# Attention with always-kept keys, then an FFN, on one core: one product per pair of heads for the kept keys

## The chip, the cores and the metric

One core of a Trainium2 chip. The metric is device time in microseconds (us) of one execution of the whole program. Before the change the median of 3 runs is 654.59 us (654.31 to 654.69).

## What is computed

Attention over 4 batches, 8 heads, 768 positions, head size 64, in fp32, where a query sees the keys of a window of 128 positions back from itself and, always, the first `n_sink` = 4 keys of the sequence (the kept keys). Then an FFN over the 3072 tokens:

```python
keep = is_sink | in_window
a = softmax(where(keep, scale * q @ k.T, -1e9))
x = (a @ v) laid out as [B * S, H * D]       # 3072 x 512
h = x @ w_in                                  # 512 -> 2048
g = h * clip(h + 3, 0, 6) / 6
out = g @ w_out                               # 2048 -> 512
```

## The kernel before

**Tiling.** The work is cut into 12 units of 256 positions (4 batches, 3 units each) and 4 pairs of heads, so 48 slots, each a pair of heads in a unit. The first 16 slots are the first units of the four batches. They have no earlier keys and so no separate kept keys, and run by an order written out by hand (`FIRST`, L734) together with loading the FFN's weights. The other 32 slots, called pairs below, run by the list `ORDER` (L858), one round of it per slot; stages of up to three slots are in work at once, as in a software pipeline. The letter f in `ORDER` takes the next step of the FFN for two units that are already done.

```python
ORDER = "f s f c00 c01 k c10 f e0 q c11 f e1 f l v d0 f f d1 f"
```

TensorE gets its instructions in this order. In this part the builder orders VectorE and ScalarE by what is ready, earlier steps first.

**Precision.** Products that need full fp32 precision are made from fp32r parts: a value is split into a high part and the rest (`split_parts`, L27, one copy and one subtraction), and the products of the parts are added up in PSUM.

**A pair's steps.** c (L385) makes four score products sp (head 0 or 1, two tiles of 128 queries each); for each VectorE's custom reduction (L382) reads sp out of PSUM, adds the mask and takes the smallest. ScalarE makes the exponentials with their sums (L419), VectorE the reciprocals (L444, L445), POOL joins two blocks (L461), ScalarE normalizes (L407). For the second head VectorE also copies the probabilities of the kept keys of both heads, high and low parts, into `ssc` (L470). d (`D_pt`, L484) transposes a head's probabilities on TensorE into pt, splits them into ph (copy on ScalarE, subtraction on VectorE, L35 and L30), and POOL masks the parts (L507, L509).

s (`D_snk`, L512) transposes `ssc` into PSUM (spt), from where ScalarE copies two blocks of 64 rows x 128 columns into `pz` (L521). The rest of `pz` is zero and stays so: POOL cleared it once (L224, in `later_constants`). Rows 0 to 63 of `pz` go with the first 128 queries, rows 64 to 127 with the second; in either half the rows hold high and low parts for both heads.

e (`E_av`, L533) multiplies one head's ph by the value parts. The 128 stationary columns `vsl` are that head's value parts, high in columns 0 to 63 and low in 64 to 127, so the result av[:, 0] has the high values' share on rows 0 to 63 and the low values' share on rows 64 to 127; av[:, 1] holds what the low probabilities add. Four matmuls (256 columns each) do that, and a fifth adds the kept keys: `sinks(p)[:, vsl]` by `pz` (L557). Then ScalarE copies rows 64 to 127 into the result x (L561) and VectorE adds the other two parts, 64 rows each (L562, L563).

`sinks(p)` (L234) holds the kept keys' values for a pair of heads, 4 x 64 columns: high and low parts of both heads, split from `raw_s` (`sink_loads`, L239; 16 times, once per batch and pair of heads). Its 128 rows are 8 groups of 16 kept keys, where a group has the values of one head and zeros for the other.

**The FFN between.** A step f is half a first product hps (six matmuls of 512 columns, L688, in `two_product`; the second half is followed by the activation on ScalarE and VectorE, L620 to L634), or a second product (`two_second`, L691; six matmuls, L698) into the sums o of a unit. With 8 f per slot, 8 slots take the 64 steps of two units.

**PSUM.** All PSUM tiles of the stretch come from one pool `ps` of eight banks (L58), under one tag, "bank". A tile has its bank from its first matmul until its last reader is done. The four sums o (two units, two tiles of 128 rows) are held from their first second product to the output, nearly all of eight slots. All others (sp, pt, spt, av, hps) take turns in the banks that are left.

After the last pair the FFN of the last two units runs alone. At the end a branch, not taken with these inputs, covers other window sizes.

Of the kernel before, what the change touches and what calls it, by code (L numbers as in the profile page):

```python
# [9 lines left out]
F32 = mybir.dt.float32  # L10
F32R = mybir.dt.float32r
# [3 lines left out]
ALU = mybir.AluOpType  # L15
# [3 lines left out]
P = 128  # L19
SK = 16  # L20
# [6 lines left out]
def split_parts(nc, hi, lo, src, hi_engine, lo_engine):  # L27

    copy_r(nc, hi_engine, hi, src)
    lo_engine.tensor_tensor(out=lo, in0=src, in1=hi.bitcast(F32), op=ALU.subtract)  # L30


def copy_r(nc, eng, out, src, scale=1.0):
    if eng is nc.scalar:
        nc.scalar.mul(out=out, in_=src, mul=scale)  # L35
    elif eng is nc.gpsimd:
        nc.gpsimd.tensor_scalar(out=out, in0=src, scalar1=scale, scalar2=1.0, op0=ALU.mult, op1=ALU.mult)
    elif scale != 1.0:
        nc.vector.tensor_scalar(out=out, in0=src, scalar1=scale, scalar2=None, op0=ALU.mult)
    else:  # L40
        nc.vector.tensor_copy(out=out, in_=src)  # L41
# [3 lines left out]
def attn_ffn_kernel(ctx: ExitStack, tc: tile.TileContext, qx, kx, vx, px, vsx, limits, w_in, w_out, out):  # L45
    nc = tc.nc
    B, NU, NP = qx.shape[0:3]
    NT, DM = out.shape
    NFP = w_in.shape[0]
    H, D, UT = 2 * NP, 64, 256  # L50
# [6 lines left out]
    work = fast.enter_context(tc.tile_pool(name="work", bufs=2))  # L57
    ps = fast.enter_context(tc.tile_pool(name="ps", bufs=8, space=PSUM))  # L58
# [53 lines left out]
    def outside(dst, src, limit):  # L112
        nc.vector.tensor_scalar(out=dst, in0=src, scalar1=limit, scalar2=-BIG, op0=ALU.is_ge, op1=ALU.mult)
# [101 lines left out]
    pz = work.tile([P, UT], F32R, name="pz", bufs=1)  # L215

    def later_constants():

        nc.gpsimd.tensor_copy(out=m_t0[:, P:2 * P], in_=ownb)
        outside(m_t0[:, 2 * P:W2], colf[:, 0:SK], ns_f)  # L220
        nc.gpsimd.tensor_copy(out=m_t1[:, 0:P], in_=m_t0[:, 0:P])
        nc.gpsimd.tensor_copy(out=m_t1[:, P:P + SK], in_=m_t0[:, 2 * P:W2])
        nc.gpsimd.tensor_copy(out=m_t1[:, P + SK:W2], in_=m_t0[:, P:2 * P])
        nc.gpsimd.memset(pz.bitcast(F32), 0.0)  # L224

    kept = {}

# [5 lines left out]

    def sinks(p):  # L234
        if "vs" not in kept:
            kept["vs"] = work.tile([P, NP, 4 * D], F32R, tag="w0", name="vs", bufs=1)
        return kept["vs"][:, p]

    def sink_loads(s):  # L239
        b, u, p = pus[s]  # L240
        if p == 0:
            kept["raw_s"] = work.tile([P, NP, 2, D], F32, name="raw_s", bufs=1)
            nc.sync.dma_start(out=kept["raw_s"], in_=vsx[b])
        v4 = sinks(p).rearrange("p (h d) -> p h d", h=4)
        split_parts(nc, v4[:, 0::2, :], v4[:, 1::2, :], kept["raw_s"][:, p], nc.scalar, nc.vector)

    SSE = "DD"
    START = 9
# [22 lines left out]
    def plain(s):  # L271
        return s < NF32 and pus[s][1] == 0
# [83 lines left out]
    def by_tile(x):  # L356

        return x.rearrange("p (a s t) -> p a t s", s=2, t=P // 2)
# [63 lines left out]
    def R_plain(s):  # L422
        d = st_[s]
        nc.vector.tensor_scalar(out=d["sm"], in0=d["av"][:, :, D], scalar1=1e-9, scalar2=None, op0=ALU.add)
        nc.vector.reciprocal(out=d["rc"], in_=d["sm"])

    def U_plain(s):
        d = st_[s]
        d["rows"] = work.tile([P, 2, 2, D], F32, tag="tmp", name="rows", bufs=1)
        nc.vector.tensor_tensor(out=d["rows"].rearrange("p t h d -> p h t d"),  # L430
                                in0=d["av"][:, :, 0:D].rearrange("p (h t) d -> p h t d", h=2),
                                in1=d["rc"].rearrange("p (h t) -> p h t", h=2).unsqueeze(3).to_broadcast([P, 2, 2, D]),
                                op=ALU.mult)

    def V_plain(s):
        d = st_[s]
        d["xp"] = ps.tile([P, UT], F32, tag="bank", name="xp")
        for t in range(2):
            nc.tensor.transpose(out=d["xp"][:, t * P:(t + 1) * P],
                                in_=d["rows"][:, t].rearrange("p h d -> p (h d)"), identity=ident)  # L440
# [71 lines left out]
    def D_snk(s):  # L512
        b, u, p = pus[s]
        if not u:
            return
        d = st_[s]
        sp = ps.tile([P, 512], F32, tag="bank", name="spt")
        nc.tensor.matmul(out=sp[:, 0:P], lhsT=ssc, rhs=ident_r, start=True, stop=True)
        for t in range(2):
            rows = slice(4 * SK * t, 4 * SK * (t + 1))  # L520
            nc.scalar.copy(out=pz[rows, t * P:(t + 1) * P], in_=sp[rows, 0:P])  # L521

    def E_plain(s, h):
        d = st_[s]
        if h == 0:
            d["av"] = ps.tile([P, 4, D1], F32, tag="bank", name="av")
        for t in range(2):
            for slot in range(t + 1):
                c = (t + slot) * P
                nc.tensor.matmul(out=d["av"][:, 2 * h + t, :], lhsT=d["pf"][:, h, c:c + P], rhs=d["VS"][:, slot, h, :],  # L530
                                 start=(slot == 0), stop=(slot == t))

    def E_av(s, h):  # L533
        b, u, p = pus[s]
        d = st_[s]
        VS = d["VS"]
        ops = [(1, P, 0, UT), (0, 0, 0, P), (2, 3 * P, P, UT)] if u else [(0, 0, 0, UT), (1, 2 * P, P, UT)]
        if plain(s):
            E_plain(s, h)
            if h == 1:  # L540
                R_plain(s)
                U_plain(s)
                V_plain(s)
                x_high(s, d["xp"])
            return

        av = ps.tile([P, 2, UT], F32, tag="bank", name="av")
        vsl = slice(2 * D * h, 2 * D * (h + 1))
        seq = []
        for slot, c, o0, o1 in ops:  # L550
            if o1 - o0 == P:
                r = d[f"pt{h}"][:, :, c:c + P].rearrange("p r (s t) -> p r t s", s=2)
                seq.append((VS[:, slot, vsl], r, av[:, :, o0:o1]))
            else:
                seq += [(VS[:, slot, vsl], by_tile(d[f"pt{h}"][:, r, c:c + UT]), av[:, r, :]) for r in range(2)]
        if u:
            seq.append((sinks(p)[:, vsl], by_tile(pz), av[:, 0, :]))  # L557
        for j, (l, r, o) in enumerate(seq):
            nc.tensor.matmul(out=o, lhsT=l, rhs=r, start=(j == 0), stop=(j == len(seq) - 1))  # L559
        rows = x_whole(s)[D * h:D * (h + 1)]  # L560
        nc.scalar.copy(out=rows, in_=av[D:P, 0, :])  # L561
        nc.vector.tensor_tensor(out=rows, in0=av[0:D, 1, :], in1=rows, op=ALU.add)  # L562
        nc.vector.tensor_tensor(out=rows, in0=av[0:D, 0, :], in1=rows, op=ALU.add)  # L563

    def in_rows(x):

        return x.rearrange("p (a t s) -> p a t s", s=2, t=P // 2)

    def x_whole(s):
        if "xf" not in kept:  # L570
            kept["xf"] = work.tile([P, 2 * NP, UT], F32, tag="sb0", name="xf", bufs=1)
        return kept["xf"][:, s % (2 * NP)]
# [15 lines left out]
    def x_high(s, src):  # L588
        if s < 2 * NP:
            copy_r(nc, weng(XHF, s), in_rows(x_two(s)[:, 0, s // NP % 2]), by_tile(src))  # L590
        else:
            copy_r(nc, weng(XHF, s), in_rows(x_whole(s)), by_tile(src))
# [217 lines left out]
    def first_step(step):  # L810
        kind, *n = step.split(".")
        n = [int(x) for x in n]
        if kind == "i":
            keep_busy(n[0], ident)
        elif kind == "m":
            later_constants()
        elif kind == "M":
            S_least(*n, st_[n[0]]["sp", n[1], n[2]])
        elif kind == "x":
            x_high(n[0], st_[n[0]]["xp"])  # L820
        elif kind == "y":
            x_low(n[0], st_[n[0]]["xp"])
        elif kind == "b":
            x_split(*n)
        elif kind in pair:
            pair[kind](*n)
        else:
            unit_step(kind, *n)
# [32 lines left out]
    def order(s):  # L861
# [3 lines left out]
        return steps  # L865

    STEPS = {"l": A_kq, "v": A_v, "k": B_k, "q": B_q, "d": D_pt, "s": D_snk, "e": slot_E}

    queues.append(two_steps(1))
# [32 lines left out]
    with tc.If(flag == 1):  # L902
        with ExitStack() as gen:
# [76 lines left out]
            with tc.For_i(0, B, 1) as bi:  # L980
                for u in range(NU):
                    xn = gp.tile([P, NP, UT], F32, name="xn")
                    for c in range(NP):
                        nc.sync.dma_start(out=xn[:, c, :],
                                          in_=xv[ds(bi, 1), :, c, u * UT:(u + 1) * UT].rearrange("o p s -> (o p) s"))
# [73 lines left out]
```

## Time and profile before

| | |
|---|---|
| median of 3 runs | 654.59 us (654.31 to 654.69) |
| the profiled execution | 655.52 us |
| its span, first to last instruction | 653.8 us |
| TensorE busy (matmul) | 642.1 us, 98% |
| VectorE busy | 506.8 us, 78% |
| ScalarE busy | 399.6 us, 61% |
| POOL busy | 180.0 us, 28% |

PE is TensorE's matmul row, PEld its weight loads (each matmul has one), DVE is VectorE, ACT ScalarE, SP the queue that issues the transfers. L12 is line 12 of the kernel. In a timeline a row is a run of like instructions: start, duration, engine, line, operation, out<-in, shapes, count, and in brackets the idle time of the engine ahead of it with what ended that. Matmuls overlap: the duration of one is longer than the time until the next starts. The share of a whole span hides that stages differ; the stage in which the changed code runs is what counts.

### The profile page before, as it was taken

What the parts mean: (1) busy time and instruction counts of PE and PEld (TensorE: products, weight loads), DVE (VectorE), ACT (ScalarE), POOL (GpSimd) and SP (SyncE); (2) the same over time, 40 slices, a digit from 0 to 9 for tenths busy, and PEclk for the clock granted to TensorE, in tenths of its full rate; (3) what the DMA queues carried; (4) which work ended last, traced back from release to release, by engine and by line L of the source; (5) the groups of instructions that cost most, each with busy time, mean ns of one, the idle gap of its engine ahead of it and who ended that gap; (6) DMA issues with size and microseconds to landing.
All of it is one profiled execution on the core that took longest, in us unless ns stands there. A gap on an engine that the chain in (4) does not pass through costs nothing.

```text
span 653.8 us, 11574 instructions
## 1 busy us (share of the span) xinstructions
PE 642.1 (98%) x3556; PEld 574.6 (88%) x3556; DVE 506.8 (78%) x1353; ACT 399.6 (61%) x982; POOL 180.0 (28%) x336
## 2 busy tenths in 40 slices
PE   8999999999999999999999999999999999999996
PEld 7898988888888888899998999999899999888885
DVE  5999999957887888887889888879897887533331
ACT  4977778645776778766667766667866665311111
POOL 1000000002454354354444444544454344000000
PEclk9999999999999999999999999999999999999999
DMA  8455930017664656544454645444744440100001
GB/s 323 190 183 208 388 149 1 2 53 211 170 175 123 170 138 197 146 122 120 116 144 120 188 127 144 118 121 122 205 116 120 109 116 2 65 1 1 0 1 69
DMA packets 45749, 82.93 MB, mean 127 GB/s; under 512 B 7024, under 2 KB 30832, under 8 KB 43632
## 3 DMA queue, kind: packets, MB, share of 16 engines
q1 hardware_dynamic: 45680, 82.11, 43.1%
q8 instruction: 31, 0.51, 0.3%
q14 instruction: 38, 0.31, 0.1%
HBM read 41.19 MB, written 6.29 MB: 73 GB/s over the span
## 4 chain that ended last, share of the span: by engine, by line
PE 86%; ACT 4%; DVE 3%; DMA 2%; SPq 1%; issue 1%; POOL 1%; ACTq 0%; DVEq 0%; POOLq 0%
PE o L698 34%; PE hps L688 33%; PE av L559 5%; PE sp L400 4%; PE av L530 2%; PE pt L494 2%; PE sp L369 2%; PE o L643 2%; PE pt L476 1%; DMA vr<-in_vx_dram 1%; DMA qr<-in_qx_dram 1%; ACT Pt L407 1%; ACT Ph L417 1%; SPq L335 1%; PE idle L86 1%
## 5 line engine op out<-in xcount | busy, mean ns | idle before, releaser
L688 PE MATMUL hps<-x,w 128*128 128x512 f32 x1104 | 263.8, 383 | 0.0
L698 PE MATMUL o<-w,gh 128*128 128x512 f32 x736 | 223.9, 384 | 0.0
L688 PEld LDWEIGHTS hps<-x,w 128*128 128x128 f32 x1104 | 200.9, 189 | 25.2 <-ACT xf L35 0.3
L698 PEld LDWEIGHTS o<-w,gh 128*128 128x128 f32 x736 | 137.4, 197 | 11.2 <-issue 0.3
L698 PE MATMUL o<-w,g 128*128 128x512 f32 x368 | 139.7, 380 | 0.0
L461 POOL TENSOR_TENSOR Pt<-Pt 128x256 f32<-128x256 f32 x64 | 53.7, 839 | 276.3 <-ACT Pt L419 276.2
L620 ACT ACTIVATE ost<-hps,three 128x512 f32<-128x512 f32 x80 | 54.8, 685 | 83.4 <-PE hps L688 82.8
L625 DVE SCALAR_TENSOR_TENSOR ost<-ost,hps 128x512 f32<-128x512 f32 x80 | 54.5, 682 | 54.7 <-ACT ost L620 54.4
L507 POOL TENSOR_SCALAR_AFFINE_SELECT ph<-ph 128x256 fp32r<-128x256 f32 x128 | 66.6, 521 | 55.3 <-ACT ph L35 55.2
L698 PEld LDWEIGHTS o<-w,g 128*128 128x128 f32 x368 | 72.4, 197 | 7.0
L419 ACT ACTIVATE Pt<-Pt,nb 128x272 f32<-128x272 f32 x128 | 65.8, 515 | 19.7 <-DVE nb L382 16.7
L382 DVE CUSTOM_DVE_ANT_0 Pt<-sp,m_t 128x272 f32<-128x272 f32 x128 | 53.1, 431 | 25.8 <-PE sp L400 22.9
L509 POOL TENSOR_SCALAR_AFFINE_SELECT ph<-ph 128x256 fp32r<-128x256 f32 x128 | 61.0, 477 | 37.2 <-DVE ph L30 29.3
L407 ACT ACTIVATE Pt<-Pt,rc 128x144 f32<-128x144 f32 x128 | 46.2, 407 | 30.4 <-DVE rc L445 20.1
L634 DVE TENSOR_TENSOR g<-ost,gh 128x512 fp32r<-128x512 f32 x80 | 57.6, 720 | 2.6
L400 PE MATMUL sp<-K 128*128 128x272 f32 x256 | 41.8, 281 | 1.3 <-DVE ph L30 0.6
L400 PEld LDWEIGHTS sp<-K 128*128 128x128 f32 x256 | 37.6, 190 | 4.2 <-DVE ph L30 1.5
L559 PEld LDWEIGHTS av<-ph,VS 128*128 128x128 f32 x256 | 38.0, 190 | 3.6 <-issue 0.7
L559 PE MATMUL av<-ph,VS 128*128 128x256 f32 x256 | 39.1, 275 | 0.0
L41 DVE CAST gh<-ost 128x512 fp32r<-128x512 f32 x80 | 37.2, 465 | 2.4
L444 DVE TENSOR_SCALAR sm<-sm 128x2 f32<-128x2 f32 x64 | 27.4, 428 | 9.3 <-ACT Pt L419 9.1
L35 ACT ACTIVATE ph<-pt 128x256 fp32r<-128x256 f32 x64 | 24.3, 384 | 16.4 <-PE pt L494 15.6
(106 smaller groups left out, 848.1 us busy)
## 6 DMA issues: line engine op xcount, KB each, us to landing
K<-kt SPq DMA_DIRECT2D x128, 200.0 KB, 3.5
K<-kt SPq DMA_DIRECT2D x128, 64.0 KB, 2.5
kr<-in_kx_dram SPq DMA_DIRECT2D x32, 200.0 KB, 2.5
vr<-in_vx_dram SPq DMA_DIRECT2D x32, 192.0 KB, 2.6
out_dram<-ost SPq DMA_DIRECT2D x22, 256.0 KB, 2.5
lent<-in_w_in_dram SPq DMA_DIRECT2D x5, 1024.0 KB, 9.0
qr<-in_qx_dram SPq DMA_DIRECT2D x40, 128.0 KB, 2.4
lent<-in_w_out_dram SPq DMA_DIRECT2D x5, 1024.0 KB, 8.7
```

What stands on the lines that cost most here:

```text
L382: nc.vector.tensor_tensor_reduce(out=cell(s, h, t, 0, w), in0=sp[:, 0:w], in1=m[:, 0:w], scale=-SCALE, scalar=3.0e38, op0=ALU.add, op1=ALU ...
L400: nc.tensor.matmul(out=sp[:, 0:w], lhsT=Q[:, h, t * P:(t + 1) * P], rhs=keys, start=(r == 0), stop=(r == 1))
L419: nc.scalar.activation(out=blk, in_=blk, func=AF.Exp, scale=-1.0, bias=d["nb"][:, i:i + 1], accum_out=d["sm"][:, i:i + 1])
L461: nc.gpsimd.tensor_tensor(out=both, in0=both, in1=prior, op=ALU.add)
L507: nc.gpsimd.affine_select(out=prior[i], in_=own[i], pattern=[[0, 2], [-1, P]], base=0, channel_multiplier=1, compare_op=ALU.is_gt, fill=0.0)
L509: nc.gpsimd.affine_select(out=own[i], in_=own[i], pattern=[[0, 2], [1, P]], base=0, channel_multiplier=-1, compare_op=ALU.is_ge, fill=0.0)
L559: nc.tensor.matmul(out=o, lhsT=l, rhs=r, start=(j == 0), stop=(j == len(seq) - 1))
L620: nc.scalar.activation(out=gf, in_=hp, func=AF.Relu, bias=three, scale=1.0)
L625: nc.vector.scalar_tensor_tensor(out=gf, in0=gf, scalar=6.0, in1=hp, op0=ALU.min, op1=ALU.mult)
L634: nc.vector.tensor_tensor(out=g, in0=gf, in1=gh.bitcast(F32), op=ALU.subtract)
L688: nc.tensor.matmul(out=state["h", j], lhsT=l(j // 2)[:, c, fs], rhs=r, start=(c == 0 and k == 0), stop=(c == NP - 1 and k == 2))
L698: nc.tensor.matmul(out=acc, lhsT=l[:, tt * P:(tt + 1) * P], rhs=r(j // 2)[:, j % 2, :].rearrange("p (s d) -> p d s", s=2), start=(j == 0 a ...
```

## The change

The two products that add the kept keys, one per head, become one for the pair of heads. `pz` is filled in full: its upper 64 rows and its lower 64 rows get the same probabilities (four copies of 64 x 128 in place of two, and no clearing). The stationary values are stacked: rows 0 to 63 hold the high parts, rows 64 to 127 the rest, 128 columns for both heads. So one matmul of 256 columns gives both heads' share, into a PSUM tile of its own, `sv`, after the second head's four matmuls. VectorE adds `sv` to the pair's whole result, 128 rows x 256 columns, after the second head's two adds.

```diff
@@ later_constants
-        nc.gpsimd.memset(pz.bitcast(F32), 0.0)
@@ sinks
-            kept["vs"] = work.tile([P, NP, 4 * D], F32R, tag="w0", name="vs", bufs=1)
+            kept["vs"] = work.tile([P, NP, 2 * D], F32R, tag="w0", name="vs", bufs=1)
@@ sink_loads
-        v4 = sinks(p).rearrange("p (h d) -> p h d", h=4)
-        split_parts(nc, v4[:, 0::2, :], v4[:, 1::2, :], kept["raw_s"][:, p], nc.scalar, nc.vector)
+        whole, v = kept["raw_s"][:, p].rearrange("p h d -> p (h d)"), sinks(p)
+        copy_r(nc, nc.scalar, v, whole)
+        nc.vector.tensor_tensor(out=v[D:P], in0=whole[D:P], in1=v[D:P].bitcast(F32), op=ALU.subtract)
@@ D_snk
         for t in range(2):
-            rows = slice(4 * SK * t, 4 * SK * (t + 1))
-            nc.scalar.copy(out=pz[rows, t * P:(t + 1) * P], in_=sp[rows, 0:P])
+            for part in range(2):
+                nc.scalar.copy(out=pz[D * part:D * (part + 1), t * P:(t + 1) * P], in_=sp[D * t:D * (t + 1), 0:P])
@@ E_av
-        if u:
-            seq.append((sinks(p)[:, vsl], by_tile(pz), av[:, 0, :]))
         for j, (l, r, o) in enumerate(seq):
             nc.tensor.matmul(out=o, lhsT=l, rhs=r, start=(j == 0), stop=(j == len(seq) - 1))
+        if u and h == 1:
+            sv = ps.tile([P, UT], F32, tag="bank", name="sv")
+            nc.tensor.matmul(out=sv, lhsT=sinks(p), rhs=by_tile(pz), start=True, stop=True)
         rows = x_whole(s)[D * h:D * (h + 1)]
         nc.scalar.copy(out=rows, in_=av[D:P, 0, :])
         nc.vector.tensor_tensor(out=rows, in0=av[0:D, 1, :], in1=rows, op=ALU.add)
         nc.vector.tensor_tensor(out=rows, in0=av[0:D, 0, :], in1=rows, op=ALU.add)
+        if u and h == 1:
+            nc.vector.tensor_tensor(out=x_whole(s), in0=sv, in1=x_whole(s), op=ALU.add)
```

## Rows read from the trace of the kernel before

**Rows 1.** The page: busy time by engine, and the chain that ended last.
```profile
PE 642.1 (98%) x3556; PEld 574.6 (88%) x3556; DVE 506.8 (78%) x1353; ACT 399.6 (61%) x982; POOL 180.0 (28%) x336
...
PE 86%; ACT 4%; DVE 3%; DMA 2%; SPq 1%; issue 1%; POOL 1%; ACTq 0%; DVEq 0%; POOLq 0%
```

**Rows 2.** Stretches: length, then busy time (instructions) by engine, clock, DMA share, GB/s.
```profile
165.00:180.00 15.00, 14.28 (x80) 11.95 (x79) 13.22 (x45) 10.97 (x36) 5.89 (x12) 1.00 0.64 167
180.00:240.00 60.00, 57.82 (x317) 50.59 (x316) 50.81 (x150) 42.01 (x123) 27.72 (x55) 1.00 0.58 151
300.00:360.00 60.00, 60.00 (x325) 53.66 (x325) 50.80 (x145) 40.97 (x116) 26.56 (x47) 1.00 0.51 132
```

**Rows 3.** The instructions of pz: durations in ns, first and last start.
```profile
L521 ACT CAST pz<-spt x64: 240/261/263, 162.3 to 554.9; 64x128 fp32r<-64x128 f32 x64
...
L559 PE MATMUL av<-pz,vs x64: 275/275/275, 165.7 to 559.1; 128*128 128x256 f32 x64
```

**Rows 4.** Timeline of TensorE, one pair: hps to hps.
```profile
318.88 1.46 PE L688 MATMUL hps<-x,w 128*128 128x512 f32 x6
...
321.58 0.86 PE L400 MATMUL sp<-K 128*128 128x272 f32 x6
...
326.10 0.28 PE L559 MATMUL av<-pz,vs 128*128 128x256 f32 x1
326.21 1.46 PE L688 MATMUL hps<-x,w 128*128 128x512 f32 x6
...
331.85 0.38 PE L688 MATMUL hps<-x,w 128*128 128x512 f32 x1
```

**Rows 5.** Timeline of VectorE, the same pair.
```profile
322.12 0.44 DVE L382 CUSTOM_DVE_ANT_0 Pt<-sp,m_t 128x272 f32<-128x272 f32 x1 [1.18 <-PE sp L400]
...
326.11 0.07 DVE L382 DVE_READ_ACCUMULATOR2_ANT nb<- 128x1 f32 x1
...
330.14 0.43 DVE L30 TENSOR_TENSOR ph<-pt,ph 128x256 fp32r<-128x256 f32 x1
```

**Rows 6.** Timeline of ScalarE, the same pair.
```profile
320.44 0.53 ACT L521 CAST pz<-spt 64x128 fp32r<-64x128 f32 x2 [0.56 <-PE spt L518]
321.78 0.69 ACT L620 ACTIVATE ost<-hps,three 128x512 f32<-128x512 f32 x1 [0.81 <-PE hps L688]
```

**Rows 7.** Timelines of TensorE and VectorE behind a change of units.
```profile
266.20 0.59 PE L698 MATMUL o<-w,gh 128*128 128x512 f32 x2
...
266.38 0.42 DVE L563 TENSOR_TENSOR xf<-av,xf 64x256 f32<-64x256 f32 x1
```

**Rows 8.** Timelines of VectorE and TensorE: a score product that waited.
```profile
219.48 0.42 DVE L30 TENSOR_TENSOR ph<-pt,ph 128x256 fp32r<-128x256 f32 x1
...
219.95 0.50 PE L400 MATMUL sp<-K 128*128 128x272 f32 x2 [0.65 <-DVE ph L30]
```

**Rows 9.** Timeline of weight loads: the first load of hps, in three pairs.
```profile
274.24 0.19 PEld L688 LDWEIGHTS hps<-x,w 128*128 128x128 f32 x1
...
326.11 0.19 PEld L688 LDWEIGHTS hps<-x,w 128*128 128x128 f32 x1
...
534.11 0.19 PEld L688 LDWEIGHTS hps<-x,w 128*128 128x128 f32 x1
```

**Rows 10.** Timeline of VectorE: the end of the fourth L382 in two of these pairs.
```profile
274.73 0.07 DVE L382 DVE_READ_ACCUMULATOR2_ANT nb<- 128x1 f32 x1
...
534.12 0.07 DVE L382 DVE_READ_ACCUMULATOR2_ANT nb<- 128x1 f32 x1
```

**Rows 11.** Timelines of VectorE and TensorE in the early stretch.
```profile
213.54 0.07 DVE L382 DVE_READ_ACCUMULATOR2_ANT nb<- 128x1 f32 x1
...
234.90 0.38 PE L688 MATMUL hps<-x,w 128*128 128x512 f32 x1
...
235.88 0.07 DVE L382 DVE_READ_ACCUMULATOR2_ANT nb<- 128x1 f32 x1
```

## The prediction

> **What bounds the kernel now.** I read the page's busy table and the chain first. TensorE is busy 98% of the span, and the chain runs through it for 86% [rows 1]. The table by stretches says where: from 240 us to 600 us it has no idle time, and before that, from 165 to 240 us, it loses 2.9 us; VectorE is busy 85 to 88% there, ScalarE 70 to 73%, and the clock is granted in full [rows 2]. The changed code runs from 165 to 559 us [rows 3], so most of it lies where every TensorE column counts. Last I read the timelines of one pair, TensorE beside VectorE and ScalarE [rows 4 to 6]: one pair takes 331.85 - 318.88 = 12.97 us, without a gap on TensorE.
>
> **Removed on TensorE.** 64 products with the kept keys become 32. One has a duration of 275 ns [rows 3], but the next matmul starts 0.11 us after it: 326.10 to 326.21 [rows 4]. By durations 32 of them would be 8.8 us, by starts 32 x 0.11 = 3.5 us; starts count, since matmuls overlap. The Trainium skill (Perfetto Trace Analysis, Identifying the Most-Contended Engine) also says that pipelining makes matmul busy time a poor measure; by its caution the saving is the 3.5, and the trace agrees. So if nothing else moved, the kernel would take 654.59 - 3.5 = 651.1 us.
>
> **Added on VectorE.** One add of 128x256 from PSUM per pair. The row nearest to it is the split of ph, also 128x256 from PSUM: 0.43 us [rows 5], as much as a 64-row add has (0.41) [rows 7]. These are the two bounds, and 0.41 is taken, as most of such adds and splits have it: 32 x 0.41 = 13.1 us more. VectorE idles 1.18 us per pair before the first score reduction [rows 5], so the steady pairs hide it; if that cover were gone the whole 13.1 would show. Queued behind the add are the ph split and the activation's L625. What they write goes into products of the next pair and of the unit half after next, several microseconds later, and the bank that the ph split reads has 2.6 us until spt takes it at about 333.1 (331.85 and six matmuls); so nobody on TensorE waits for the 0.41.
>
> **Added on ScalarE.** Four copies into pz for two: 2 x 0.26 = 0.52 us per pair, 16.7 us in all. In the pair shown they would end at 321.5 instead of 320.97, before the activation at 321.78, for which ScalarE waits 0.81 us anyway [rows 6]. Zero there. The bank of spt comes free with them, at 321.5. Its next user is the third score product, the third two of the six matmuls that start at 321.58, at 0.115 us each so at 322.04 [rows 4]: covered too, by 0.5 us. pz itself is read by the second head's product, over 4 us later.
>
> **No change.** The value parts keep 16 copies and 16 subtractions of as many columns (the subtractions on half the rows): zero, covered by the same idle times. POOL, busy 28% [rows 1], loses one clearing ahead of the whole stretch: I take 0. No DMA is moved or issued.
>
> **The bank that sv takes.** This decides. All PSUM tiles share eight banks. Four are held by the second layer's sums o for a whole unit pair, so the other four rotate: per pair av (first head), the fourth score product, av (second head), hps, two pt, hps, spt and three score products. In the program that the kernel builds, a new tile gets the bank that was released longest ago, and its first weight load waits for that bank's last reader. Such a wait is in the trace already: at 219.95 a score product, which uses nothing of ph, waited 0.65 us for VectorE's ph split, and started 0.05 us after that ended (219.48 + 0.42) [rows 8].
>
> Now, after the second head's products, hps takes the bank of the third score product, which was read some 2 us before. After the change sv is in front of it and takes that bank, and hps gets the next: that of the fourth score product, whose reader L382 ends at 326.11 + 0.07 = 326.18 [rows 5]. The weight load of hps started at 326.11 [rows 9] and could start at 325.99 with one matmul gone; it will start at 326.18 + 0.05 = 326.23. The 0.11 us saved is lost, and 0.13 us more. L382 does not come earlier with it: VectorE works without a gap from 322.12, when it gets the first score product, and the removed matmul lies behind that. So each such pair should grow from 12.97 to about 13.10 us.
>
> The Trainium skill (Perfetto Trace Analysis, Optimization Strategy) says that the same gap repeating on the engine that should be saturated can mean that the next tile finds no SBUF or PSUM. It gives no price; without the rule the sum is 651.1, with it that of the next paragraph. Row and rule agree on the wait at 219.95.
>
> **The sum.** In 18 of the 32 pairs a product of the first layer stands right behind the second head. In 14 of them the load of hps is 0.08 to 0.09 us ahead of the end of L382, as at 326.11 against 326.18 and, the last, at 534.11 against 534.12 + 0.07; in the four others 0.56, 0.24, 0.43 and 0.15 ahead, the most at 274.24 against 274.80 [rows 5, 9, 10]. With 0.05 us of delay: 14 x 0.13 + 0.61 + 0.29 + 0.48 + 0.20 = **+3.4 us**.
> In the three pairs behind a change of units the last new o moves on to the second head's av bank: at 266.20 it starts, and the reader L563 ends at 266.80 [rows 7], so with the delay of 0.05 and the 0.11 by which a weight load precedes its matmul it would start at 266.96, 0.76 later; the two like it come to 0.26 and 0.45 by the same subtraction. That pause lets VectorE catch up, so the 0.61, 0.29 and 0.48 shrink towards 0.13: 1.5 - 1.0 = **+0.5 us**.
> The first seven pairs: the products at 212.27 and 234.90 would move on to banks that L382 frees at 213.61 and 235.95 [rows 11], 1.3 and 1.1 us after the start of these products. The first is mostly swallowed by waits that follow (0.65 us at 219.95 among them). Bounds: -0.8 (seven times 0.11, no wait) to +3.0 (both, and some of the VectorE and ScalarE work that covers less in this stretch). I take **+1.0**, nearest to the second wait alone.
> The three pairs at a change of units and the last one keep the gain: 4 x 0.11 = **-0.4 us**.
> Sum: 3.4 + 0.5 + 1.0 - 0.4 = +4.5 us, some 0.7%. The profiled execution took 655.52 us (span 653.8), 0.9 over the median of 654.59; the 4.5 goes on the median: **659.1 us**.
>
> **Rivals.** (a) *The wait does not come*: the bank behind hps is another, or L382 moves ahead of the first head's adds by one add (0.33 us) and the load of hps no longer meets it. For: nothing in the trace of before shows the bank order beyond single waits, and VectorE's order is chosen anew when the work changes. Against: the margin is already negative in all 18 pairs. Then 651.1 plus 0 to 2 us from the early stretch: 651.1 to 653.1, say 651.7. Chance 0.15.
> (b) *Give and take*: the waits come in the early stretch and at the changes of units alone, or are about as long as the matmul removed. For: 0.13 us is thin, an end of L382 0.1 us sooner halves it. 653.3 to 655.9, say 654.6. Chance 0.12.
> (c) *VectorE becomes the bound*: this decides from the point where it has no idle time left before the first score reduction, 1.18 us per pair; then its 13.1 us show, less the 3.5: 664.2. For: 88% busy early. Against: 0.41 is a third of that idle time. Chance 0.08.
> The forecast has 0.65, of which 0.03 lies within the margin; its own range is 655.9 to 662, from the lower bound of the early stretch and thinner waits, to both early waits in full.
>
> **Chances and range.** The measurement can tell about 0.2%, 1.3 us, from no change. Faster: (a), 0.15. Same: (b) and 0.03, 0.15. Slower: 0.62 + 0.08 = 0.70. The range 653.2 to 663.0 leaves out (a), and a little of (c).
>
> **What would show it.** Right: pz products x32; among TensorE's waits, product loads (L688) waiting for L382 in about 18 pairs, 0.2 us each; pairs of 13.1 us in the 300 to 360 us stretch; VectorE 13 us and ScalarE 17 us busier. Wrong: pairs of 12.86 us (12.97 less 0.11) without TensorE idle time: then (a). Pairs well over 13.2 us with VectorE never waiting for a score product: then (c). No wait at hps, but one at pt or at the later o: the bank order was misread.

## The result, and the profile after

The changed kernel takes 664.21 us against 654.59 us, both medians of five runs: a ratio of 1.0147, 95% interval 1.0133 to 1.016. One of its five runs, of 2359.63 us, was disturbed; the other four took 663.19 to 664.53 us, with a median of 663.97. It is **slower by 9.6 us** (9.4 by those four); 659.1 was predicted, with a range up to 663.0. The profiled execution took 663.72 us.

First the page of the changed kernel: busy time by engine and the chain that ended last, as in [rows 1].
```profile
PE 644.4 (97%) x3524; PEld 571.1 (86%) x3524; DVE 511.1 (77%) x1385; ACT 415.7 (63%) x1046; POOL 182.3 (28%) x335
...
PE 75%; DVE 10%; ACT 5%; DMA 5%; issue 2%; SPq 1%; POOL 0%; ACTq 0%; DVEq 0%; POOLq 0%
```
TensorE runs 32 matmuls fewer and is a smaller part of the chain: 75%, from 86%. ScalarE is busy 16.1 us longer, about the 16.7 worked out; VectorE is busy only 4.3 us longer, where the prediction's sign was 13, though the 32 adds last 13.2 by themselves. They overlap with their neighbours (at 359.44 and 359.77 below, the next instruction starts 0.33 us after an add of 0.41), and other instructions got shorter, above all the 32 splits of VS, the value parts: 17.8 us in all, from 21.7.

Where TensorE lost time: first the stretches (columns as in [rows 2]), then its waits (us in total, times, longest).
```profile
180.00:240.00 60.00, 57.35 (x310) 49.19 (x309) 53.05 (x158) 44.05 (x133) 28.45 (x56) 1.00 0.58 151
240.00:300.00 60.00, 58.32 (x314) 51.65 (x313) 49.71 (x143) 43.63 (x126) 24.86 (x44) 1.00 0.50 140
300.00:360.00 60.00, 59.67 (x319) 53.18 (x318) 51.75 (x149) 41.39 (x121) 25.72 (x43) 1.00 0.50 127
360.00:420.00 60.00, 58.30 (x313) 51.53 (x312) 48.27 (x138) 42.48 (x119) 27.07 (x48) 1.00 0.52 140
```
```profile
PE o L701 <- DVE xf L564: 2.3, 2, 1.1
PE pt L494 <- ACT Pt L407: 1.9, 4, 0.6
...
PE o L701 <- ACT kt L35: 1.2, 1, 1.2
...
PE hps L691 <- DVE nb L382: 0.7, 2, 0.3
```
A change of units is the place, once in eight pairs, where the FFN finishes two units and takes up the next two. The stretch from 300 to 360 us, whose change of units starts only at about 352, lost 0.33 us; those from 240 and from 360 us, with a change inside, lost 1.7 each, where TensorE never stopped before. The long waits are at o and at pt, not at hps. Waits under about 0.2 us show on the row of weight loads, where hps waits 19 times, 0.2 us each in the mean, as the prediction's sign for its bank order said:
```profile
PEld hps L691 <- DVE nb L382: 4.0, 19, 0.5
```

**Pair by pair.** I set the start of the second head's product with the kept keys (the sink product) beside that in the kernel before, for all 32 pairs. A steady pair is one behind the eighth that is neither at a change of units nor right behind it. By the eighth pair the changed kernel's profile is 1.1 us ahead; at the last one, 567.3 against 559.1 [rows 3], it is 8.2 us behind. Between:

| step | pairs | each | in all |
|---|---|---|---|
| right behind the three changes of units | 3 | +2.07, +2.26, +2.20 | +6.5 |
| steady, a first-layer product behind the second head | 15 | +0.12 to +0.19 | +2.1 |
| like these, but more | 3 | +0.48, +0.48, +0.30 | +1.3 |
| at the three changes of units (gain kept, once more than the 0.11 saved) | 3 | -0.12, -0.33, -0.11 | -0.6 |

The 8.2 is the difference of the two profiled executions (663.72 - 655.52), the 9.6 that of the medians. A second profile of the same early program (run e14 below) reaches the eighth pair 1.3 us sooner than the profile of before; against it the changed kernel is 0.2 us behind there.

**A steady pair**: timelines of TensorE, the weight loads and VectorE, as in [rows 4, 5, 9].
```profile
314.72 0.28 PE L560 MATMUL sv<-pz,vs 128*128 128x256 f32 x1
314.97 1.56 PE L691 MATMUL hps<-x,w 128*128 128x512 f32 x6
```
```profile
314.97 1.16 PEld L691 LDWEIGHTS hps<-x,w 128*128 128x128 f32 x6 [0.17 <-DVE nb L382]
```
```profile
314.84 0.07 DVE L382 DVE_READ_ACCUMULATOR2_ANT nb<- 128x1 f32 x1
```
hps starts 0.25 us after sv instead of 0.11, and its six matmuls last 1.56 us instead of 1.46, as the second is late: 0.24 lost, 0.11 saved, **+0.13 as forecast**. The load waited for the end of L382 (314.91) plus 0.06.

**A change of units.** The kernel before, timelines of ScalarE and VectorE:
```profile
356.85 0.42 ACT L35 ACTIVATE x<-xf 128x256 fp32r<-128x256 f32 x1 [0.72 <-DVE xf L563]
357.17 1.07 ACT L656 ACTIVATE ost<-o 128x512 f32<-128x512 f32 x2
...
360.28 0.60 ACT L656 ACTIVATE ost<-o 128x512 f32<-128x512 f32 x1
...
361.68 0.68 ACT L620 ACTIVATE ost<-hps,three 128x512 f32<-128x512 f32 x1
```
```profile
356.40 0.42 DVE L563 TENSOR_TENSOR xf<-av,xf 64x256 f32<-64x256 f32 x1
...
362.39 0.69 DVE L625 SCALAR_TENSOR_TENSOR ost<-ost,hps 128x512 f32<-128x512 f32 x1
```
The changed kernel, 1.68 us later by then: ScalarE, VectorE, TensorE.
```profile
359.88 0.42 ACT L35 ACTIVATE x<-xf 128x256 fp32r<-128x256 f32 x1 [1.33 <-DVE xf L566]
360.20 1.07 ACT L659 ACTIVATE ost<-o 128x512 f32<-128x512 f32 x2
...
363.31 0.60 ACT L659 ACTIVATE ost<-o 128x512 f32<-128x512 f32 x1 [0.91 <-DMA out_dram<-ost]
363.94 0.53 ACT L521 CAST pz<-spt 64x128 fp32r<-64x128 f32 x2
...
365.40 0.69 ACT L623 ACTIVATE ost<-hps,three 128x512 f32<-128x512 f32 x1
```
```profile
358.06 0.42 DVE L564 TENSOR_TENSOR xf<-av,xf 64x256 f32<-64x256 f32 x1
...
359.44 0.41 DVE L566 TENSOR_TENSOR xf<-sv,xf 128x256 f32<-128x256 f32 x1
359.77 0.41 DVE L30 TENSOR_TENSOR ph<-pt,ph 128x256 fp32r<-128x256 f32 x1
...
366.12 0.69 DVE L628 SCALAR_TENSOR_TENSOR ost<-ost,hps 128x512 f32<-128x512 f32 x1 [2.07 <-ACT ost L623]
```
```profile
369.35 0.63 PE L494 MATMUL pt<-ident_r,Pt 128*128 128x128 f32 x2 [0.56 <-ACT Pt L407]
...
374.59 0.68 PE L701 MATMUL o<-w,gh 128*128 128x512 f32 x2 [1.14 <-DVE xf L564]
```
Read it downwards.

- The copy of the unit's last x stands on ScalarE and needs the pair's whole result. It waited for L563, and now waits for the added L566: 359.88 against 356.85 + 1.68, **1.35 us late**. L564, the former L563, is on time (358.06 against 356.40 + 1.68). Three other instructions that the builder put ahead of the add take 0.96 us, the add itself 0.41.
- Behind the x copy on ScalarE stand the copies out of the last sums (ost<-o), kt, the four pz copies, and only then the activation: 365.40 against 361.68 + 1.68, 2.0 us late, with the two more pz copies in it. The late x copy is passed on in full although ScalarE is idle for 0.91 us in between. The third copy out of the sums waits for the output transfer of the first, and starts 3.11 us after that copy in either kernel (357.17 to 360.28, 360.20 to 363.31).
- VectorE stands idle 2.07 us for the activation, where it waited for nothing. What is behind it there (the last two L382, the softmax) comes late to the transposes pt, and L564 late to the last new o, whose bank it frees.

At the first change of units the row of o names kt on ScalarE as what ended the wait (1.2 us in the list above). kt is not read from PSUM, and L564 ends at 267.09, 0.15 us ahead of o, as it does at the two others, so I take L564 to be the releaser there too. VectorE and TensorE:
```profile
266.67 0.42 DVE L564 TENSOR_TENSOR xf<-av,xf 64x256 f32<-64x256 f32 x1
...
267.24 0.68 PE L701 MATMUL o<-w,gh 128*128 128x512 f32 x2 [1.16 <-ACT kt L35]
```

### The profile page after: what moved, and what is told of

It is laid out like the page before. It is cut to its first block, busy times and chain, and to the rows that moved or that the text cites. A ratio compares the mean times of both kernels' runs of the same rounds, so it can differ in the third digit from the quotient of the medians.

```text
span 661.9 us, 11583 instructions
## 1 busy us (share of the span) xinstructions
PE 644.4 (97%) x3524; PEld 571.1 (86%) x3524; DVE 511.1 (77%) x1385; ACT 415.7 (63%) x1046; POOL 182.3 (28%) x335
## 4 chain that ended last, share of the span: by engine, by line
PE 75%; DVE 10%; ACT 5%; DMA 5%; issue 2%; SPq 1%; POOL 0%; ACTq 0%; DVEq 0%; POOLq 0%
PE hps L691 29%; PE o L701 27%; PE av L530 3%; PE sp L400 3%; PE av L557 3%; PE sp L369 2%; PE pt L476 2%; DMA vr<-in_vx_dram 2%; PE o L646 2%; DVE Pt L382 2%; PE pt L494 1%; PE hps L612 1%; DMA out_dram<-ost 1%; ACT Pt L407 1%; DVE sm L444 1%
## 5 line engine op out<-in xcount | busy, mean ns | idle before, releaser
L507 POOL TENSOR_SCALAR_AFFINE_SELECT ph<-ph 128x256 fp32r<-128x256 f32 x128 | 67.4, 527 | 45.6 <-ACT ph L35 45.6
L382 DVE CUSTOM_DVE_ANT_0 Pt<-sp,m_t 128x272 f32<-128x272 f32 x128 | 53.3, 432 | 28.0 <-PE sp L400 26.8
L509 POOL TENSOR_SCALAR_AFFINE_SELECT ph<-ph 128x256 fp32r<-128x256 f32 x128 | 63.6, 498 | 40.6 <-DVE ph L30 32.6
L407 ACT ACTIVATE Pt<-Pt,rc 128x144 f32<-128x144 f32 x128 | 46.2, 407 | 21.7 <-DVE rc L445 20.6
L521 ACT CAST pz<-spt 64x128 fp32r<-64x128 f32 x128 | 33.1, 258 | 23.2 <-PE spt L518 21.9
L41 DVE CAST gh<-ost 128x512 fp32r<-128x512 f32 x80 | 35.6, 445 | 2.3
```

The source lines that it names most:

```text
L382: nc.vector.tensor_tensor_reduce(out=cell(s, h, t, 0, w), in0=sp[:, 0:w], in1=m[:, 0:w], scale=-SCALE, scalar=3.0e38, op0=ALU.add, op1=ALU ...
L407: nc.scalar.mul(out=blk, in_=blk, mul=c)
L507: nc.gpsimd.affine_select(out=prior[i], in_=own[i], pattern=[[0, 2], [-1, P]], base=0, channel_multiplier=1, compare_op=ALU.is_gt, fill=0.0)
L509: nc.gpsimd.affine_select(out=own[i], in_=own[i], pattern=[[0, 2], [1, P]], base=0, channel_multiplier=-1, compare_op=ALU.is_ge, fill=0.0)
```

## The experiments

B is the theory of the prediction, that the banks alone cost; Q adds ScalarE's queue, the order of its instructions, at the changes of units. Times are medians, beside the kernel before on the same chip (654.1 to 654.4 us).

**e1_no_add**: VectorE's add is left out (the kept keys' share never reaches the result).
```diff
-        if u and h == 1:
-            nc.vector.tensor_tensor(out=x_whole(s), in0=sv, in1=x_whole(s), op=ALU.add)
```


> Leaves out VectorE's add of sv, so the kept keys' share is missing from the result; all else is the changed kernel. Two theories of the 9.6 us. B (banks alone): sv pushes the product hps and, at the three changes of units, the last sum o onto banks that come free late; the add plays no part, since the bank of hps is that of the fourth score product: 663 to 664 us, steady pairs still 0.13 us longer than before, each change of units still 2.2 us. Q (queue at the change of units): there ScalarE's copy of the last pair's x stands still for the new add and everything behind it, the activation among them, comes later, and with it VectorE and the last o: without the add each change of units gives back about 1.0 to 1.4 us: 660 to 661 us, steady pairs unchanged at +0.13.


660.40 us, ratio 1.0098 (1.0082 to 1.0115): Q. Most steady pairs keep +0.13. A change of units with the pair behind it falls to 0.6 to 1.0 us, from 2.2 to 2.4. But with no reader sv's bank comes free at once, which turns the banks there (hps waits now, o no longer), so this alone doesn't separate the two.

**e2_two_copies**: two pz copies in place of four, and the clearing put back (half of pz stays zero: of the kept keys' values one tile gets only the high parts, the other only the rest).
```diff
-            for part in range(2):
-                nc.scalar.copy(out=pz[D * part:D * (part + 1), t * P:(t + 1) * P], in_=sp[D * t:D * (t + 1), 0:P])
+            nc.scalar.copy(out=pz[D * t:D * (t + 1), t * P:(t + 1) * P], in_=sp[D * t:D * (t + 1), 0:P])
```


> Two copies into pz in place of four, one per half, and the clearing put back: half of the kept keys' share is left out. B: 663 to 664 us, nothing changes. Q: the two copies (0.53 us) stand ahead of the activation in ScalarE's queue at each change of units, so each gives back about 0.5 us: 662 to 663 us; steady pairs unchanged at +0.13, since there ScalarE waits anyway.


661.16 us, 1.0107 (1.009 to 1.0124): below what either said, nearer to Q. At the changes of units pt starts 0.05 to 0.15 us late instead of 0.7, and the two pairs of +0.48 go back to 0.13; the wait at the last o stays (1.3 to 1.4 us).

**e3_bank_alone**: both edits, so that of the change only the product and its bank remain (the kept keys' share is left out).


> No add and two copies: what is left of the change on the path is one matmul less and the bank that sv takes (the kept keys' share is left out of the result). B: 663 to 664 us. Q: only what the bank costs remains: 18 pairs at +0.13 (2.3 us), the last o at each change of units 0.3 to 0.8 us, less some 1 us that the early stretch gains: 655.5 to 658 us.


659.11 us, 1.0075 (1.0059 to 1.0092), between the two: +4.8 us for a bank that nobody reads, the saved product in it. As in e1 the banks turn: two of the changes of units cost 0.5 us or less with the pair behind them, the one at 360 us 2.2. So this is not the bank's cost in the changed kernel, where the add reads sv.

**e4_sv_behind_f**: the whole change, with product, addition and the split of x moved behind the next first-layer step.
```diff
-    ORDER = "f s f c00 c01 k c10 f e0 q c11 f e1 f l v d0 f f d1 f"
+    ORDER = "f s f c00 c01 k c10 f e0 q c11 f e1 f g l v d0 f f d1 f"
```


> The whole change, but the product into sv, its add and the split of x stand one FFN step later, behind the first half of hps. Then hps gets the bank of the third score product again, as before the change. Both theories: no wait at hps, steady pairs 12.86 us (0.11 below before) in place of 13.10, so 18 x 0.24 = 4.3 us less than the changed kernel. B: the last o is left, 658 to 660 us. Q: 659 to 661 us, each change of units still 2 us or more longer, as the add comes no sooner.


659.32 us, 1.0077 (1.006 to 1.0094): both allow it. All but two of the steady pairs turn to -0.11, so their +0.13 was the bank of hps; the changes of units keep 2.1 to 3.3.

**e7_before_4_copies, e8_before_add**: ScalarE's load, and the later x, each without any bank, on the kernel before.
```diff
+            for _ in range(2):
                 nc.scalar.copy(out=pz[rows, t * P:(t + 1) * P], in_=sp[rows, 0:P])
```
```diff
+        if u and h == 1:
+            nc.vector.tensor_scalar(out=x_whole(s), in0=x_whole(s), scalar1=1.0, scalar2=None, op0=ALU.mult)
```


> The kernel before with each of its two copies into pz made twice: ScalarE's load of the change without its bank and without its addition. If ScalarE's queue at the changes of units costs by itself (Q), about 0.45 us at each of the three and 0.5 us at two other pairs: 655.5 to 657 us. If only the bank costs (B): 654 to 655 us.

> The kernel before with one more VectorE operation on the pair's whole x (times 1.0, in place), where the changed kernel adds: the copy of the last pair's x on ScalarE waits for it, and no bank and no copy is added. If that wait is what puts the activation late at the changes of units (Q), 0.7 to 1.5 us at each of the three: 656.5 to 659 us. If only the bank costs (B): 654 to 655 us.


656.19 us, 1.0031 (1.0018 to 1.0043), and 656.21 us, 1.0032 (1.0021 to 1.0042): **each costs 2.1 us by itself**, e8 a little less than Q said. The profile of e7 is of its fastest run and shows 1.2 of its 2.1. The operation in e8 lasts 0.29 us, the add 0.41. B alone is out. In e7 the waits are not at pt, where the changed kernel has them, but at a score product that waits for the last pz copy and so, I take it, has spt's bank; at three of the four an x copy stands between the pz copies. Its waits, then its timeline of ScalarE and TensorE:
```profile
PE sp L400 <- ACT pz L522: 1.4, 4, 0.4
```
```profile
346.56 0.42 ACT L35 ACTIVATE x<-xf 128x256 fp32r<-128x256 f32 x1
347.00 0.26 ACT L522 CAST pz<-spt 64x128 fp32r<-64x128 f32 x1
...
347.31 0.50 PE L400 MATMUL sp<-K 128*128 128x272 f32 x2 [0.41 <-ACT pz L522]
```
In e8 the chain is that of the changed kernel, shorter: timelines of ScalarE and VectorE, and TensorE's wait at the next change.
```profile
357.13 0.42 ACT L35 ACTIVATE x<-xf 128x256 fp32r<-128x256 f32 x1 [1.37 <-DVE xf L565]
...
362.67 0.69 DVE L627 SCALAR_TENSOR_TENSOR ost<-ost,hps 128x512 f32<-128x512 f32 x1 [0.69 <-ACT ost L622]
...
476.06 1.10 PE L690 MATMUL hps<-x,w 128*128 128x512 f32 x4 [0.51 <-DVE xf L563]
```
With e3 the three make 4.8 + 2.1 + 2.1 = 9.0 of the 9.6 us. This is a check of size and no more, as e3's bank has no reader and each of the three is known to 0.7 to 1.1 us.

**e10_x_copy_vector, e14_before_vector**: three x copies go to VectorE, in the changed kernel and, as a control, in the kernel before.
```diff
-            copy_r(nc, weng(XHS, s), x[:, 0, one], x_whole(s))
+            copy_r(nc, nc.vector if s % (2 * NP) == 2 * NP - 1 else weng(XHS, s), x[:, 0, one], x_whole(s))
```


> The changed kernel, but the copy of each unit's last x is VectorE's instead of ScalarE's (three copies that count), so that nothing on ScalarE stands behind the added addition. If the wait in ScalarE's queue is the cause at the changes of units (Q), they fall from 2.2 us to 0.5 to 1.0 each: 659 to 661 us. If the bank is (B), nothing changes: 663 to 664.5 us.

> Control: the kernel before with the same three x copies on VectorE. Its changes of units have 0.5 us of waits in all, so both theories say 653.5 to 654.8 us; a gain here would have to be taken off what e10 and e12 show.


e10: 658.86 us, 1.0063 (1.0047 to 1.008). It is 4.8 us over the kernel before on its chip: **three copies moved give back half of the 9.6 us**, where B expected nothing. The changes of units fall to 0.8 each: the wait at pt is gone, that at the last o is left (kt named for one of the three, as before). e14: 654.27 us, 1.000 (0.9991 to 1.0009), so the move is worth nothing where no addition stands ahead of it. What is left in e10, TensorE's waits:
```profile
PE o L701 <- DVE xf L564: 1.4, 2, 0.7
...
PE o L701 <- ACT kt L35: 0.8, 1, 0.8
```

**e5_sv_in_pt**: sv gets no bank; it goes into the unused half of the next pair's first pt.
```diff
-            sv = ps.tile([P, UT], F32, tag="bank", name="sv")
-            nc.tensor.matmul(out=sv, lhsT=sinks(p), rhs=by_tile(pz), start=True, stop=True)
...
+        if h == 0 and "sv" in kept:
+            sv_product(kept["sv"], pt[:, UT:2 * UT])
```


> The whole change, but the stacked product has no bank of its own: it goes into the unused half of the next pair's first transposes, one FFN step later (the last pair keeps a bank). All other products take the banks that they took before. The ScalarE copy of the last pair's x still waits for the added addition, and later than in the changed kernel. If at the changes of units it is ScalarE's queue alone that costs (Q), those three keep about 2 us each and only the 24 later pairs go from +0.13 to -0.11: 657.5 to 659.5 us. If it takes a bank that comes free late as well (B), they fall below 1 us each: 653 to 656 us.


657.50 us, 1.0048 (1.0032 to 1.0065). Nearly all steady pairs stand at -0.11 (two at +0.06 and +0.23), and no o waits any more: that was the bank. The queue is left, at the lower edge of what Q said: at two of the changes 0.9 us at pt and 0.56 at the next hps. TensorE's waits:
```profile
PE pt L494 <- ACT Pt L407: 2.5, 7, 0.6
...
PE hps L703 <- ACT kt L35: 0.8, 2, 0.4
```

**e12_pt_vector**: e5 and e10 together.


> As e5, and the copy of each unit's last x is VectorE's instead of ScalarE's (three copies that count): neither a bank of its own nor anything on ScalarE behind the added addition. Q: the waits left at e5's changes of units (1.1 to 1.5 us each) go, 653.5 to 656 us. If they have another cause: 657 to 658 us.


654.70 us, 1.001 (1.0001 to 1.0019). The changes of units cost 0.5 us at most: Q again, and within 0.2% of the kernel before.

The changed kernel, e10, e5 and e12 are the four cases with and without the bank, with and without the wait in ScalarE's order: 9.6, 4.8, 3.4 and 0.3 us over the kernel before. Moving the three copies gives back 4.8 us with the bank and 3.1 without; doing without the bank gives back 6.2 us with the wait and 4.5 without. Without the bank the product also stands one step later. All adds and all four pz copies are still in e12, whose changes of units cost 0.5 us at most: by itself neither VectorE's nor ScalarE's load costs more there.

**e11_pt_one_copy, e13_pt_one_copy_vector**: e5 and e12 with a pz filled by one ScalarE copy, for which VectorE writes the sink columns twice and TensorE transposes them by two products.
```diff
-        nc.tensor.matmul(out=sp[:, 0:P], lhsT=ssc, rhs=ident_r, start=True, stop=True)
+        for t in range(2):
+            nc.tensor.matmul(out=sp[:, t * P:(t + 1) * P], lhsT=ssc[:, t * P:(t + 1) * P], rhs=ident_r, start=True, stop=True)
...
+        copy_r(nc, nc.scalar, pz, sp[:, 0:UT])
```


> As e5 (the stacked product in the unused half of the next pair's first transposes), and pz is filled by one ScalarE copy instead of four: VectorE writes the sink columns twice, and TensorE transposes them by two products instead of one (one more of 64 ns per pair, +2.0 us). ScalarE's load for pz falls below that of the kernel before. If the queue on ScalarE is what is left at e5's changes of units (Q: 0.9 at the transposes, 0.55 at the next hidden product), these fall by half or more: 656 to 658 us. If ScalarE's load does not matter there, only the added product shows: 659 to 660 us.

> Both edits of e11 and e12 on e5. Q: no wait left at the changes of units, the added transposing product still costs 2.0 us: 655 to 657 us. If the waits have another cause: 658 to 660 us.


660.81 us, 1.0097 (1.0082 to 1.0112), and 659.55 us, 1.0081 (1.0068 to 1.0095): the first is slower than either theory said, the second where "another cause" put it. The added transposing product costs 0.11 us per steady pair, not 0.064 (they stand at 0.00, e5's at -0.11), and in the early stretch it waits for VectorE. TensorE's timeline in a steady pair of e11, and its waits:
```profile
323.05 0.34 PE L538 MATMUL spt<-ident_r,ssc 128*128 128x128 f32 x2
323.22 1.51 PE L704 MATMUL hps<-x,w 128*128 128x512 f32 x6
```
```profile
PE spt L538 <- DVE xf L579: 2.0, 2, 1.0
...
PE spt L538 <- DVE ssc L472: 1.5, 2, 0.8
```
So the two times say little on ScalarE's load. The traces say more: at the changes of units e11 has no wait at pt left, and e13 no wait over 0.2 us at all, as Q said.

**e15_late_pt**: e12, but the first seven pairs give sv a bank of its own, as the changed kernel does.
```diff
+        if h == 1 and (s < PT_FROM or s == NS - 1):
+            kept["own"] = ps.tile([P, UT], F32, tag="bank", name="sv")
+            sv_product(s, kept["own"])
```


> As e12, but the first seven pairs give the stacked product a bank of its own, as the changed kernel does; the later pairs put it into the next pair's first transposes. In e12 the second head's sink product of the eighth pair starts 2.75 us later than in e14 (the kernel before in all but three copies), in the changed kernel 0.2 us later. If it is the place of the product in these seven pairs that costs e12 its gain (theory E), this run gains about 2.5 us on it: 651.5 to 653 us, faster than the kernel before. If the early stretch comes out as in e12 whatever the place (ScalarE's two more copies, the addition): 654 to 655.5 us.


**652.53 us, 0.9973 (0.9965 to 0.9982): faster than both kernels**, by 1.7 us on the one before. Using pt's half in those seven pairs cost e12 about 2 us; whether by the later place of the product or by the add that then holds pt's bank isn't separated, as e15 changes both. The 2.75 us of the expectation was too much as a measure: in e12 the product itself stands 1.43 us later in its pair (326.13 to 327.56, below). Timelines of TensorE, two steady pairs of e12:
```profile
326.13 1.46 PE L703 MATMUL hps<-x,w 128*128 128x512 f32 x6
327.42 0.38 PE L494 MATMUL pt<-ident_r,Pt 128*128 128x128 f32 x2
327.56 0.36 PE L517 MATMUL pt<-pz,vs 128*128 128x256 f32 x1
...
340.42 0.36 PE L517 MATMUL pt<-pz,vs 128*128 128x256 f32 x1
```
One pair is 340.42 - 327.56 = 12.86 us, the time that the prediction gave for a pair without waits. In e15's page TensorE is back at its share of the span, and its chain at 85%:
```profile
PE 638.0 (98%) x3524; PEld 569.0 (88%) x3524; DVE 514.1 (79%) x1390; ACT 414.2 (64%) x1041; POOL 179.3 (28%) x335
...
PE 85%; DVE 6%; ACT 3%; DMA 3%; issue 2%; SPq 1%; POOL 0%; DVEq 0%; ACTq 0%
```

## Why the prediction was right in direction and too small

- **The saving**: right. 0.11 us per product by starts, not 0.275; e4, e5, e12 and e15 show -0.11 per pair wherever nothing waits.
- **The bank that sv takes**: right in the steady pairs, to the hundredth in 13 of the 18. +3.4 was forecast for the 18 pairs, less 1.0 for the catch-up; they measured +3.3 (2.05 + 1.26). The catch-up came (0.13 behind the changes of units), but three pairs lost 0.30 to 0.48; two of these go back to 0.13 in e2 and in e10. That e3 gives +4.8 against the +4.5 of the sum is luck: 2.2 us of it are lost at a single change of units. The Trainium skill (Perfetto Trace Analysis, Optimization Strategy) says that an equal gap that repeats can mean a missing buffer; the trace agrees, 0.24 us on TensorE in 13 pairs, but the larger loss was in three places only.
- **The first seven pairs**: +1.0 forecast, 0.2 measured against e14's profile, and two profiles of the same program differ by 1.3 there. The term was not shown, and is too small to be judged in one profile.
- **The step that failed: "Zero there" for ScalarE, and "nobody on TensorE waits for the 0.41" for VectorE.** Both were read off one steady pair [rows 5, 6] and said of all. At three of the 32 pairs, each the last of two units, the next work on ScalarE is the copy of the last x, which reads what the added addition writes; it stands at the head of ScalarE's order, ahead of an activation that VectorE waits for. The x copy came 1.35 us late, the activation 2.0, and TensorE lost 2.07 to 2.26 us each time. With those three copies off ScalarE 4.8 of the 9.6 us are gone (e10); on the kernel before a later x alone costs 2.1 us (e8), the two more copies 2.1 (e7).
- **Behind the changes of units**: the term of the sum that this step made too small, +0.5 forecast and +6.5 measured. The waits at the last o were foreseen (0.76, 0.26 and 0.45 us) at the right product with the right reader, but came to 1.3 to 1.4 us each, as that reader stood behind the late activation; with the x copy off ScalarE they are 0.9 to 1.0 (e10), still more than forecast. The waits at pt, 0.9 us each with the late second matmul, were not foreseen at all.
- **Rivals**: (a) and (b) fell with the steady pairs. (c) named the right time, 664.2, by luck, and the range up to 663.0 left out that time. Its reason is wrong: VectorE still waits for score products, 26.8 us in all ahead of L382, and is busy 77%:
```profile
L382 DVE CUSTOM_DVE_ANT_0 Pt<-sp,m_t 128x272 f32<-128x272 f32 x128 | 53.3, 432 | 28.0 <-PE sp L400 26.8
```

What stays open: what makes the 0.3 us between steady pairs of 0.13 and of 0.48, which both e2 and e10 take away; why the waits at o in e10 are still about twice the forecast in the mean; and whether bank and queue cost more together than apart. The four cases give 1.7 us for that, which is no more than their intervals together. No run took away the output transfer that the third copy out of the sums waits for, or put the add ahead of the three instructions that delay it.

## What to carry to other kernels

Cost an added instruction at every place where it runs, not in one steady iteration: look for the place where a different reader of its result stands first in an engine's order, and follow that order to what stands behind the reader. A new PSUM tile costs not only its own bank but shifts who takes which; putting it into the unused half of a tile that is there anyway took that cost away in the steady pairs and at o, but in the first seven pairs it cost about 2 us. And a saving that a new wait hides comes out again once the wait is gone: here three copies on another engine and a half-empty bank turned +1.5% into -0.3%.

## What was not expected of the hardware

A second transposing matmul of 128 columns cost as much as a product of 256 (0.11 us by starts): 323.22 - 323.05 = 0.17 us for two in e11, where one takes 0.06, here in e12, so 0.11 for it. Why is not shown.
```profile
320.31 0.23 PE L535 MATMUL spt<-ident_r,ssc 128*128 128x128 f32 x1
320.37 1.50 PE L703 MATMUL hps<-x,w 128*128 128x512 f32 x6
```
And two more copies of 0.26 us per pair on an engine that is idle over a third of the span cost 2.1 us (e7), where a later product waited for the last of them; in e12, with as many pz copies and three x copies off ScalarE, no such wait is left behind the eighth pair.
